# Gelu's tiles lent to MLP results, accumulator copies in halves, denominators spread a turn later, and TensorE's hand-over waits placed when due

## The chip, the cores and the metric

The kernel runs on one core of one Trainium2 chip. A core has a matrix engine (TensorE, PE in the profile, with its weight loads as PEld), a vector engine (VectorE, DVE), a scalar engine (ScalarE, ACT), GpSimd (POOL) and a sync engine (SyncE, SP), each with its own instruction queue that runs in order, and 16 DMA engines that move data between memory and the on-chip SBUF. TensorE writes to PSUM, which has 8 banks of 512 fp32 columns.

The metric is device time in microseconds of one execution. Of the kernel before there are three timed runs, and one more execution that was profiled.

## The reference

For x of 2048 tokens by 448 channels the reference computes an attention block and an MLP block on the same input and mixes them by a gate. Cut to what matters:

```python
def _A_ref(x, wqkv, wo):                 # S=2048, D=448, H=16 heads of Dh=28
    qkv = (x @ wqkv).reshape(B, S, 3, H, Dh)...
    scores = einsum("bhqd,bhkd->bhqk", q, k) * (Dh ** -0.5)
    p = softmax(scores)
    return einsum("bhqk,bhkd->bhqd", p, v)... @ wo

def _B_ref(x, w1, b1, w2, b2):           # F=1792
    y = layernorm(x)
    h = gelu(y @ w1 + b1)
    return h @ w2 + b2

g = sigmoid((x * gate_w).sum(-1, keepdims=True))
return g * _A_ref(x, ...) + (1 - g) * _B_ref(x, ...)
```

All of it is fp32. The kernel splits an operand a into a high part (rounded to a fast format, fp32r) and a low part a - high, and computes a product of two operands as high x high + high x low + low x high.

## The kernel before

**Two stages.** The first stage (class `Strips`, up to about 451 us) computes q, k, v, then the MLP, and beside them begins the row maxima of the attention scores. The second stage (from the loop over `turn_of`) computes scores, exponentials, the products with v, the projection and the mix.

**The strip stage.** TensorE's 128 rows are used as four row groups of 32 rows, "strips", that work side by side. Work is cut into pieces: `QK` and `Val` (q, k, v), `Up` (128 of the 1792 hidden channels for a block of 512 tokens) and `Down` (128 tokens of an MLP result). The 2048 tokens are four column blocks c = 0 to 3; in each 14 Up pieces are followed by 4 Down pieces. A piece owns one PSUM bank and must be visited once by each of the four strips, one after the other, since all four add into the same bank. The loop `run` is a planner: it keeps a planned time `t[s]` for each strip, takes the strip with the least time, and writes out one product at a time, with planned costs (0.232 us for a product of 512 columns, 0.204 for one of 448). This fixes the order of TensorE's instructions.

**Hand-overs.** When a strip has finished its visit, `end` lets SP increase a semaphore `hand` by one once the visit's last product is done, and keeps the count as `x.sig`. The piece counts as ready for another strip `HOP` = 0.6 us after the planned end (`x.ready`). The next strip's first product of that piece waits for `hand >= x.sig` (lines 486 and 487). SP's queue also holds DMA issues, and is in order.

**Row maxima.** Between these products each strip computes score products for the row maxima (line 212): 128 queries by 512 keys into bank 6 or 7, which VectorE then reduces (line 214). There are 1024 of them; those that the strip stage has no room for are done in attention by `lone`, up to three in a turn.

**Closing a piece.** `Up.close` lets ScalarE compute Gelu into a tile `h` (two buffers) and round it into `hh`; GpSimd then forms the low part `hl` out of `h` and `hh`. `Down.close` lets ScalarE copy the bank into a tile (line 398) and issue a transfer of it to the memory tensor `gbs` (line 401). That tile is `gb`, with two buffers; for the last two results of the last column block alone it is a tile of Gelu's `h`. The last strip of a first Up piece is held back while Down pieces of the block before are open.

**Attention.** The 16 heads are four groups g of four heads, the queries four blocks c of 512: n = 4g + c counts 16 accumulations. A turn computes five to seven units (128 keys by 512 queries of one head: three products each, line 1166), lets ScalarE take the exponential of them in two portions (line 1170), inserts row maxima (`lone`), then runs what the agenda holds for that turn, then products with v (line 1178) into bank 7. In a turn of five units the row maxima stand at three places: the first in bank 6, the second in another bank, the third in bank 6 again; in a turn of six there are two, both in bank 6. When the last product of an accumulation n has been placed, `valued` calls `finish_a`: VectorE copies bank 7 into `ob` (line 1026), and SP issues a transfer that brings the four rows of denominators into a small tile `lt`. Two turns later `finish_b` lets VectorE take reciprocals, and SP issues a store of them to memory and four transfers that spread them over 32 rows each (`rc`). Two turns after that `finish_c` lets GpSimd multiply `ob` by `rc`. The last accumulation goes another way (`finish_last`).

Of the kernel before, what the change touches and what calls it, by code (L numbers as in the profile page):

```python
# [15 lines left out]
P = 128  # L16
# [3 lines left out]
DH = 28  # L20
F = 1792
NG = 4
CH = 512
NC = S // CH
# [11 lines left out]
def kernel(ctx: ExitStack, tc: tile.TileContext, xt, wqk, wv, wo, xk, w1, b1, w2, b2,  # L36
                          ident_d, sel_d, out):
    nc = tc.nc
# [21 lines left out]
    rls = dram.tile([NG * NC, 4, CH], F32, name="rls")  # L60
# [101 lines left out]
    class RowMax:  # L162
# [64 lines left out]
        def close(self, n):  # L227
            mf, mt = self.mf[n % 2], self.mt[n % 2]
            nc.vector.reduce_max(mf[:, 0:16], self.mx[n % 2].rearrange("p j i k -> p (j i) k"), axis=AX)
            nc.vector.transpose(mt, mf)  # L230
# [14 lines left out]
    hand = tc.alloc_semaphore("hand")  # L245
# [123 lines left out]
    class Down(Piece):  # L369
# [21 lines left out]
            return st.hready.get((self.c, f, p), 1e9) > now or self.c == 0 and st.w2ready.get(f, 1e9) > now  # L391

        def close(self, st, now):
            if self.c == NC - 1 and self.i > 1:
                gb = mhp[0].tile([P, CH], F32, name="h", bufs=2)[:, :D]
            else:
                gb = mhp[0].tile([P, D], F32, name="gb", bufs=2)
            nc.scalar.activation(gb, bk[:, self.bank, :D], AF.Copy)  # L398
            st.use("act", now + 0.2, 0.56)
            st.free[self.bank] = st.act + 0.1  # L400
            nc.scalar.dma_start(gbs[self.c * TPC + self.i], gb)
            st.use("act", now, 0.5)

    class Strips:


        def __init__(self, tiles):
            self.tiles = tiles
            self.t = [0.0] * 4
            self.visit, self.held = [None] * 4, [None] * 4  # L410
            self.feed, self.stat = Feed(self, []), Feed(self, bxr)
            self.live = []
            self.free = {b: 0.0 for b in range(6)}
            self.rm = {6: 0.0, 7: 0.0}
            self.dve = self.act = self.pool = -1.0
            self.clock = self.dma = -1.0
            self.tasks = []
            self.count = 0
            self.hot = [1e9] * 4
            self.hready, self.yready, self.xready, self.wready, self.w1ready, self.w2ready = {}, {}, {}, {}, {}, {}  # L420
            self.vready = 1e9
            self.did = {}
            self.handed = 0

        def use(self, engine, start, cost):
            setattr(self, engine, max(getattr(self, engine), start) + cost)
# [6 lines left out]
        def at(self, t, fn, **uses):  # L433
            self.tasks.append((t, self.count, fn, uses))
            self.count += 1
# [30 lines left out]
        def run(self):  # L466
            while self.tiles or self.live:
                s = min(range(4), key=lambda s: (self.t[s], s))
                now = self.t[s]
                self.run_tasks(now)  # L470
                if self.rowmax(s, now):
                    continue
                v = self.visit[s]
                if v is None or v[0].fixed and self.held[s] is None:
                    x = self.pick(s, now, v and v[0])
                    if x is not None:
                        x.busy = True
                        self.held[s] = v
                        v = self.visit[s] = [x, x.ops(s), 0]
                if v is None or v[0].lacks(self, v[2], now):  # L480
                    self.t[s] = now + 0.1
                    continue
                x, ops, m = v
                a, b = ops[m] if not x.fixed else (ops[m][0][ops[m][2]][ops[m][3], ops[m][4]], ops[m][1][ops[m][2]][ops[m][3]])
                n = b.shape[-1]
                if m == 0 and x.sig:
                    nc.tensor.wait_ge(hand, x.sig)
                mm = nc.tensor.matmul(bk[:, x.bank, :n], a, b, start=x.first, stop=(len(x.rem) == 1 and m == len(ops) - 1),  # L488
                                      skip_group_check=True)
                x.first = False  # L490
                self.t[s] = now + x.cost
                v[2] += 1
                if v[2] == len(ops):
                    self.visit[s], self.held[s] = self.held[s], None
                    self.end(x, s, mm)
# [397 lines left out]
    for i, key in enumerate(load):  # L893
        r = slots[i % 8]
# [14 lines left out]
    for b, m in enumerate((0, 3, 4)):  # L909
        x = QK(0, m)  # L910
# [32 lines left out]
    def turn_bank(i):  # L943
        return (i + shift) % 6
# [73 lines left out]

    pv = bk[:, 7]
    obs = {}  # L1020

    def finish_a(n):
        ob = ao.tile([P, CH], F32, name="ob", bufs=1)
        lt = ao.tile([P, CH // 32], F32, name="lt")
        obs[n] = ob, lt
        nc.vector.tensor_copy(ob, pv)  # L1026
        nc.sync.dma_start(lt, ob[DH:P:32, :])

    def finish_b(n):
        ob, lt = obs[n]  # L1030
        rc = ao.tile([P, CH], F32, name="rc", bufs=1)
        obs[n] = ob, rc
        nc.vector.reciprocal(lt, lt)
        r = rls[n]
        nc.sync.dma_start(r.rearrange("j (a b) -> (j a) b", b=CH // 32), lt)
        for j in range(4):
            nc.sync.dma_start(rc[32 * j:32 * j + 32], r[j].partition_broadcast(32))

    def finish_c(n):
        g, c = divmod(n, NC)  # L1040
        ob, rc = obs.pop(n)
        if g < NG - 1:
            nc.gpsimd.tensor_mul(ot[g][:, c * CH:(c + 1) * CH], ob, rc)
            return
        nc.gpsimd.tensor_mul(ob, ob, rc)
        split_o(g, c, ob)
# [53 lines left out]
    def valued(n, turn):  # L1100

        g, c = divmod(n, NC)
        if n == NG * NC - 1:
            finish_last(n)
            return
        finish_a(n)
        at(turn + 2, lambda: finish_b(n))
        at(turn + 4, lambda: finish_c(n))
        if g == NG - 1:
            for i in range(TPC):  # L1110
                tail.append((turn + 6 + i, c * TPC + i))
# [7 lines left out]
    def lone(s, b, turn):  # L1119
        if not rowmax.ready(s) or turn < cold[s]:  # L1120
            return
        for kind, n, j in rowmax.one(s, bk[:, b]):
            if kind == "q":
                at(turn + 1, lambda n=n, j=j: rowmax.load_q(n, j))
            elif kind == "k":
                at(turn + 1, lambda n=n, j=j: rowmax.load_k(n, j))
                cold[j] = turn + 5
            else:
                at(turn + 1, lambda n=n: rowmax.close(n))
                at(turn + 2, lambda n=n: rowmax.store(n))  # L1130

    def turn_of(u, turn):

        left = UNITS - u
        owed = rowmax.left()
        size = 5 if owed and owed > 2 * ((left - 104) // 6) + 6 * sixes[0] else 6
        sixes[0] = size == 6
        if not owed and not (tail and tail[0][0] <= turn + 1):
            size = 7
        size = min(left, size)  # L1140
        na = min(4 if size == 7 else 3, size)
        nb = size - na
        for x in range(u, u + size):
            n = x // 64
            if n not in begins:
                begins.add(n)
                begun(n, turn)
        extra = {5: ((0, 3, 6), (3, 1, 5), (5, 2, 6)), 6: ((0, 3, 6), (5, 2, 6))}.get(size, ())
        if size == 7:
            sevens.append(turn)  # L1150
        place = (lambda i: i) if sevens else turn_bank
        if turn in projected:
            extra = extra[1:]
        for half, first, count in ((0, 0, na), (1, na, nb)):
            for p in range(3):
                for x, o, b in extra:
                    if x == 3 * half + p:
                        lone((u + o) % 4, b if b == 6 else turn_bank(b), turn)
                for i in range(first, first + count):
                    n, k = divmod(u + i, 64)  # L1160
                    k, j = divmod(k, 4)
                    r = slice(32 * j, 32 * j + DH + (p == 0))
                    ks = slice(k * P, (k + 1) * P)
                    w = (khi, klo, khi)[p][n // NC]
                    q = (qh, qh, ql)[p][n % 3]
                    nc.tensor.matmul(bk[:, place(i)], w[r, ks], q[r], start=(p == 0), stop=(p == 2), skip_group_check=True)  # L1166
            if count:
                t = ap.tile([P, 4 - half, CH], F32, name=f"p{half}")
                b = place(first)
                nc.scalar.activation(t[:, :count], bk[:, b:b + count], AF.Exp, scale=SCALE)  # L1170
                for i in range(count):
                    prob[u + first + i] = t[:, i]
        return size

    def batch(b, turn, sl=slice(0, CH)):
# [11 lines left out]
    while b < UNITS // 4:  # L1187
# [12 lines left out]
        while 4 * b + 4 <= before and quota:  # L1200
# [7 lines left out]
            b, begun_half = b + 1, False  # L1208
# [59 lines left out]
```

## Time and profile before

| | us |
|---|---|
| median of three runs | 1082.11 |
| lowest, highest | 1080.81, 1086.48 |
| the profiled execution | 1083.55 |
| its span, first to last instruction | 1081.8 |
| TensorE busy | 1068.8 (99%) |
| VectorE busy | 740.8 (68%) |
| ScalarE busy | 634.0 (59%) |
| GpSimd busy | 368.3 (34%) |
| granted TensorE clock | 0.999 |

A row of a group reads: line of the kernel, engine, operation, tile written <- tiles read, shapes, count; then busy time in us and mean duration in ns, and the idle time of the engine just before these instructions with what ended it ("<-"). A row of a timeline begins with the start and the length in us; several merged instructions carry a count. ACTq, SPq, DVEq and PEldq are an engine's queue: DMA issues and semaphore instructions, which are not counted as busy. TensorE's busy time covers up to four row groups that run side by side, so that 99% does not mean full speed.

### The profile page before, as it was taken

Reading aid. Unit: us, or ns where it says so; the run is one execution under the profiler, and the core shown is the slowest. Engines: PE = TensorE matmul, PEld = TensorE weight load, DVE = VectorE, ACT = ScalarE, POOL = GpSimd, SP = SyncE. Lnnn points to the kernel's source line nnn. Section 1 sums busy time; section 2 is a strip of 40 time slices with the busy share of each in tenths; the row PEclk is TensorE's granted clock in tenths of the full one; section 3 lists DMA queues with packets and bytes.
Section 4 is the critical chain, followed back from the end, with each engine's and each line's share of the span. In section 5 each row is a group of like instructions: output and inputs, shape, how many; then the busy total and the mean of one; then the engine's idle time right before and its main releaser. Section 6 shows DMA issues by size and latency. Waiting matters only on the chain.

```text
span 1081.8 us, 31072 instructions
## 1 busy us (share of the span) xinstructions
PE 1068.8 (99%) x13450; PEld 725.4 (67%) x13450; DVE 740.8 (68%) x1186; ACT 634.0 (59%) x654; POOL 368.3 (34%) x388
## 2 busy tenths in 40 slices
PE   9999999999999999999999999999999999999997
PEld 6999999999999899844444444444444444464555
DVE  4899998999999999876667655676664444422102
ACT  5234463042142033288788788778888888857671
POOL 4565577336244037441001101300110332444431
PEclk9999999999999999999999999999999999999999
DMA  6696433212100104220000011310000301011111
GB/s 232 214 269 217 168 111 104 77 46 61 45 7 7 46 12 118 92 77 18 25 11 27 16 31 38 78 41 6 25 26 23 71 27 50 25 55 36 61 47 67
DMA packets 47785, 73.20 MB, mean 68 GB/s; under 512 B 13840, under 2 KB 28816, under 8 KB 46848
## 3 DMA queue, kind: packets, MB, share of 16 engines
q1 hardware_dynamic: 33888, 39.11, 12.4%
q0 software_dynamic: 5120, 16.89, 5.5%
q10 hardware_dynamic: 8640, 15.21, 3.9%
q8 instruction: 105, 1.72, 0.7%
q14 instruction: 32, 0.26, 0.1%
HBM read 51.75 MB, written 19.31 MB: 66 GB/s over the span
## 4 chain that ended last, share of the span: by engine, by line
PE 95%; ACT 2%; DMA 2%; DVE 1%; issue 1%; SPq 0%; DVEq 0%; ACTq 0%
PE bk L488 34%; PE bk L1178 22%; PE bk L1166 18%; PE bk L212 15%; PE bk L1004 1%; ACT p L1170 1%; PE bk L1005 1%; PE bk L1006 1%; DMA gbs<-gb 1%; PE bk L920 1%; DMA first<-in_xt 1%; ACT gb L398 0%; DVE ob L1026 0%; PE bk L948 0%; DVE mx L214 0%
## 5 line engine op out<-in xcount | busy, mean ns | idle before, releaser
L214 DVE TENSOR_REDUCE mx<-bk 128x1 f32<-128x512 f32 x1024 | 673.7, 688 | 221.8 <-PE bk L212 178.6
L1170 ACT ACTIVATE p<-bk 128x1536 f32<-128x1536 f32 (+1 forms) x381 | 481.1, 1315 | 125.8 <-PE bk L1166 125.1
L212 PE MATMUL bk<-kd,qd 28*128 28x512 f32 x1024 | 449.8, 441 | 0.6 <-DVE mx L214 0.2
L212 PEld LDWEIGHTS bk<-kd,qd 28*128 28x128 f32 x1024 | 186.0, 182 | 179.7 <-DVE mx L214 115.1
L488 PE MATMUL bk<-yh,w1f 32*128 32x512 f32 x1568 | 192.9, 393 | 2.2 <-ACT gb L398 2.2
L488 PE MATMUL bk<-yl,w1f 32*128 32x512 f32 x784 | 167.4, 392 | 0.0
L488 PEld LDWEIGHTS bk<-yh,w1f 32*128 32x128 f32 x1568 | 154.6, 183 | 4.9 <-ACT gb L398 3.4
L488 PE MATMUL bk<-w2h,hh 32*128 32x448 f32 x896 | 145.0, 366 | 0.0
L488 PE MATMUL bk<-w2l,hh 32*128 32x448 f32 x896 | 144.1, 363 | 0.0
L1178 PE MATMUL bk<-p,va 128*32 128x512 f32 (+1 forms) x1144 | 130.2, 556 | 0.0
L1178 PE MATMUL bk<-p,vb 128*32 128x512 f32 (+1 forms) x1184 | 129.2, 542 | 0.0
L363 POOL TENSOR_TENSOR hl<-h,hh 128x512 fp32r<-128x512 f32 x56 | 72.4, 1305 | 137.2 <-ACT hh L356 99.7
L840 POOL CAST yh<-yl 128x512 fp32r<-128x512 f32 x16 | 9.8, 611 | 288.0 <-DMA yl<-qk 131.2
L488 PEld LDWEIGHTS bk<-yl,w1f 32*128 32x128 f32 x784 | 105.8, 183 | 0.3
L488 PEld LDWEIGHTS bk<-w2l,hh 32*128 32x128 f32 x896 | 103.1, 183 | 0.3
L488 PEld LDWEIGHTS bk<-w2h,hh 32*128 32x128 f32 x896 | 102.7, 183 | 0.4
L1166 PE MATMUL bk<-yh,ka 29*128 29x512 f32 x512 | 101.1, 483 | 0.5 <-ACT p L1170 0.5
L1166 PE MATMUL bk<-yh,kb 29*128 29x512 f32 x512 | 96.5, 480 | 1.7 <-ACT p L1170 1.7
L488 PE MATMUL bk<-w2h,hl 32*128 32x448 f32 x896 | 93.1, 362 | 0.0
L398 ACT ACTIVATE gb<-bk 128x448 f32<-128x448 f32 x14 | 7.6, 545 | 136.8 <-PE bk L488 129.7
L1166 PE MATMUL bk<-yh,la 28*128 28x512 f32 x512 | 83.4, 393 | 0.0
L488 PEld LDWEIGHTS bk<-w2h,hl 32*128 32x128 f32 x896 | 82.4, 183 | 0.3
(141 smaller groups left out, 1604.5 us busy)
## 6 DMA issues: line engine op xcount, KB each, us to landing
qk<-qo ACTq DMA_DIRECT2D x28, 256.0 KB
raw<-in_xt SPq DMA_DIRECT2D x17, 256.0 KB
vs<-vt ACTq DMA_DIRECT2D x16, 256.0 KB
rc<-rls SPq DMA_DIRECT2D x60, 64.0 KB
bxr<-in_xk POOLq DMA_DIRECT2D x8, 448.0 KB, 6.4
acc<-gbs SPq DMA_DIRECT2D x16, 224.0 KB
out_y<-acc SPq DMA_DIRECT2D x16, 224.0 KB
qd<-qk SPq DMA_DIRECT2D x60, 56.0 KB
```

Source lines behind the costliest of these rows:

```text
L212: nc.tensor.matmul(ps, self.qd[n % 2][r, i * P:(i + 1) * P], self.kd[r, k * 512:(k + 1) * 512], start=True, stop=True)
L214: nc.vector.reduce_max(self.mx[n % 2][:, j, i, k:k + 1], ps, axis=AX)
L363: nc.gpsimd.tensor_sub(hl[f], h, hh[f].bitcast(F32))
L488: mm = nc.tensor.matmul(bk[:, x.bank, :n], a, b, start=x.first, stop=(len(x.rem) == 1 and m == len(ops) - 1), skip_group_check=True)
L840: nc.gpsimd.tensor_copy(h, l.bitcast(F32))
L920: nc.tensor.matmul(bk[:, b], w, v, start=(i == 0), stop=(i == len(ops) - 1), skip_group_check=True)
L1004: nc.tensor.matmul(po, h, woh[:, g], start=(g == 0), stop=False, skip_group_check=True)
L1005: nc.tensor.matmul(po, h, wol[:, g], start=False, stop=False, skip_group_check=True)
L1006: nc.tensor.matmul(po, l, woh[:, g], start=False, stop=(g == NG - 1), skip_group_check=True)
L1166: nc.tensor.matmul(bk[:, place(i)], w[r, ks], q[r], start=(p == 0), stop=(p == 2), skip_group_check=True)
L1170: nc.scalar.activation(t[:, :count], bk[:, b:b + count], AF.Exp, scale=SCALE)
L1178: nc.tensor.matmul(bk[32 * j:32 * j + 32, 7, sl], vg[n // NC][:, k, 32 * j:32 * j + 32], prob[4 * b + j][:, sl], start=(k == 0), stop=(k = ...
```

## The change

There are four parts.

1. `Down.close` takes a tile of Gelu's `h` for the third and fourth token tile (i > 1) of every column block, where before it did so in the last block alone.
2. In `run` each strip product looks for the highest `sig` among all pieces whose planned `ready` has come (and its own piece's), and waits for it if TensorE has not waited for as much before (`passed`). Before, only the first product of a visit waited, for its own piece.
3. `finish_a` copies the first 256 columns of bank 7; the other 256 and the transfer of the denominators are put off to `copy_rest`, which the next turn calls behind its first row maximum (or at the end of its scores if it has none).
4. The four spreading transfers move out of `finish_b` into `spread_rc`, one turn later.

```diff
         def close(self, st, now):
-            if self.c == NC - 1 and self.i > 1:
+            if self.i > 1:
                 gb = mhp[0].tile([P, CH], F32, name="h", bufs=2)[:, :D]
             else:
                 gb = mhp[0].tile([P, D], F32, name="gb", bufs=2)
...
-            self.handed = 0
+            self.handed = self.passed = 0
...
-                if m == 0 and x.sig:
-                    nc.tensor.wait_ge(hand, x.sig)
+                due = max((y.sig for y in self.live if y.sig and y.ready <= now), default=0)
+                due = max(due, x.sig or 0)
+                if due > self.passed:
+                    nc.tensor.wait_ge(hand, due)
+                    self.passed = due
...
+    late = []
 
     def finish_a(n):
...
-        nc.vector.tensor_copy(ob, pv)
-        nc.sync.dma_start(lt, ob[DH:P:32, :])
+        nc.vector.tensor_copy(ob[:, :CH // 2], pv[:, :CH // 2])
+
+        def rest():
+            nc.vector.tensor_copy(ob[:, CH // 2:], pv[:, CH // 2:])
+            nc.sync.dma_start(lt, ob[DH:P:32, :])
+
+        late.append(rest)
+
+    def copy_rest():
+        while late:
+            late.pop()()
 
     def finish_b(n):
...
-        r = rls[n]
-        nc.sync.dma_start(r.rearrange("j (a b) -> (j a) b", b=CH // 32), lt)
+        nc.sync.dma_start(rls[n].rearrange("j (a b) -> (j a) b", b=CH // 32), lt)
+
+    def spread_rc(n):
         for j in range(4):
-            nc.sync.dma_start(rc[32 * j:32 * j + 32], r[j].partition_broadcast(32))
+            nc.sync.dma_start(obs[n][1][32 * j:32 * j + 32], rls[n][j].partition_broadcast(32))
...
         at(turn + 2, lambda: finish_b(n))
+        at(turn + 3, lambda: spread_rc(n))
         at(turn + 4, lambda: finish_c(n))
...
                         lone((u + o) % 4, b if b == 6 else turn_bank(b), turn)
+                        copy_rest()
...
+        copy_rest()
         return size
```

The order of TensorE's products is the same before and after; only waits move. On ScalarE, at the third crossing (the Down results of column block 2, then the first Gelus of block 3), the rows of before are these; a DMAHW wait is one for a transfer, Pool one for GpSimd:

```order
L398 ACTIVATE gb<-bk 128x448 [waits DMAHW2_49,PE_49]
L401 DMA gbs<-gb 128x448 [waits DMAHW6_49,Activation_49]
L398 ACTIVATE gb<-bk 128x448 [waits DMAHW3_49,PE_49]
L401 DMA gbs<-gb 128x448 [waits DMAHW7_49,Activation_49]
L398 ACTIVATE gb<-bk 128x448 [waits DMAHW6_49,PE_49]
L401 DMA gbs<-gb 128x448 [waits DMAHW0_49,Activation_49]
L398 ACTIVATE gb<-bk 128x448 [waits DMAHW7_49,PE_49]
L401 DMA gbs<-gb 128x448 [waits DMAHW1_49,Activation_49]
L355 ACTIVATE h<-bk,b1s 128x512 [waits PE_49,Pool_49]
```

and those of after:

```order
L398 ACTIVATE gb<-bk 128x448 [waits DMAHW0_49,PE_49]
L401 DMA gbs<-gb 128x448 [waits DMAHW6_49,Activation_49]
L398 ACTIVATE h<-bk 128x448 [waits PE_49,Pool_49]
L401 DMA gbs<-h 128x448 [waits DMAHW7_49,Activation_49]
L398 ACTIVATE h<-bk 128x448 [waits PE_49,Pool_49]
L401 DMA gbs<-h 128x448 [waits DMAHW0_49,Activation_49]
L398 ACTIVATE gb<-bk 128x448 [waits DMAHW2_49,PE_49]
L401 DMA gbs<-gb 128x448 [waits DMAHW1_49,Activation_49]
L355 ACTIVATE h<-bk,b1s 128x512 [waits DMAHW7_49,PE_49]
L356 ACTIVATE hh_2908<-h 128x512 [waits Activation_49]
L355 ACTIVATE h<-bk,b1s 128x512 [waits DMAHW0_49,PE_49]
```

The third and the fourth copy no longer wait for transfers issued in the same crossing (DMAHW6 and DMAHW7); the first two Gelus now wait for two of them (DMAHW7 and DMAHW0).

On VectorE, around the end of an accumulation in attention, before (mx is the tile of row maxima, x6 means six reductions in a row):

```order
L230 STREAM_TRANSPOSE mt_158<-mf_156 128x32
L214 TENSOR_REDUCE mx_155<-bk 128x1 x33
L1026 COPY ob<-bk 128x512
L214 TENSOR_REDUCE mx_155<-bk 128x1 x6
L1033 RECIPROCAL lt<-lt 128x16
```

and after:

```order
L230 STREAM_TRANSPOSE mt_158<-mf_156 128x32
L214 TENSOR_REDUCE mx_155<-bk 128x1 x33
L1030 COPY ob<-bk 128x256
L214 TENSOR_REDUCE mx_155<-bk 128x1
L1033 COPY ob<-bk 128x256
L214 TENSOR_REDUCE mx_155<-bk 128x1 x5
L1046 RECIPROCAL lt<-lt 128x16
```

One reduction now stands between the two halves.

On TensorE, a place in the Up products of the strip stage (w1f is a split weight tile, its number names the piece; yh and yl are the parts of y), before:

```order
L212 MATMUL bk<-kd,qd_153 128x512 [waits DVE_49]
L488 MATMUL bk<-yl,w1f_1773 128x512
L488 MATMUL bk<-yh,w1f_1744 128x512
L488 MATMUL bk<-yl,w1f_1629 128x512
L488 MATMUL bk<-yh,w1f_1773 128x512
L488 MATMUL bk<-yl,w1f_1744 128x512
L488 MATMUL bk<-yh,w1f_1688 128x512 [waits hand]
```

and after (the same pieces, under numbers that are lower by one to three):

```order
L212 MATMUL bk<-kd,qd_153 128x512 [waits DVE_49]
L491 MATMUL bk<-yl,w1f_1772 128x512 [waits hand]
L491 MATMUL bk<-yh,w1f_1742 128x512
L491 MATMUL bk<-yl,w1f_1627 128x512
L491 MATMUL bk<-yh,w1f_1772 128x512
L491 MATMUL bk<-yl,w1f_1742 128x512
L491 MATMUL bk<-yh,w1f_1685 128x512 [waits hand]
```

A product in the middle of another piece's visit (1772) now waits for a hand-over that is due.

## The prediction

> **What bounds the kernel now.** I read the page first: the engines' shares and the chain of waits.
>
> ```profile
> span 1081.8 us, 31072 instructions
> PE 1068.8 (99%) x13450; PEld 725.4 (67%) x13450; DVE 740.8 (68%) x1186; ACT 634.0 (59%) x654; POOL 368.3 (34%) x388
> PE 95%; ACT 2%; DMA 2%; DVE 1%; issue 1%; SPq 0%; DVEq 0%; ACTq 0%
> ```
>
> TensorE looks like the only bound. But its 99% is made of row groups that overlap, so I split the span by stage with the table of windows (columns: stretch, length, then busy time and count of PE, PEld, DVE, ACT, POOL).
>
> ```profile
> 60.00:182.00 122.00, 122.00 (x2064) 116.91 (x2063) 113.16 (x185) 58.16 (x115) 81.08 (x89) 1.00 0.55 176
> 182.00:451.00 269.00, 266.75 (x4601) 254.44 (x4593) 261.18 (x412) 68.40 (x111) 110.18 (x96) 1.00 0.16 46
> 451.00:1000.00 549.00, 546.57 (x5415) 256.95 (x5417) 314.69 (x497) 442.71 (x356) 118.32 (x116) 1.00 0.14 39
> ```
>
> In the strip stage (to 451 us) VectorE is busy 93% and then 97% of the time with row maxima: TensorE may place the next L212 product only when VectorE has emptied one of two banks. There VectorE sets the pace, and what counts is time in which VectorE idles. In attention (from 451) it is busy 57% and TensorE sets the pace, but each turn holds a chain through one bank: L212 product, row maximum, next L212 product.
>
> **Gelu's buffers.** The copies of the Down results (L398) use two buffers `gb`; the third must wait until the first one's transfer has landed. The view of that tile (what its engine waited for, then who waited for it), and the page's row of the products that wait:
>
> ```profile
> L398 ACT ACTIVATE gb<-bk x14: 543/545/547, 207.0 to 450.0; 128x448 f32<-128x448 f32 x14
>   DMA gbs<-gb: 6.7, 4
>   PEld bk L488: 3.4, 3
> L488 PE MATMUL bk<-yh,w1f 32*128 32x512 f32 x1568 | 192.9, 393 | 2.2 <-ACT gb L398 2.2
> ```
>
> ScalarE waited four times, 6.7 us in all, and three times TensorE waited for it (2.2 us with no product running, 3.4 us by its weight loads). ScalarE's timeline at the second and third crossing from one column block to the next:
>
> ```profile
> 290.22 0.33 ACTq L401 DMA_DIRECT2D gbs<-gb  x1
> 292.90 0.54 ACT L398 ACTIVATE gb<-bk 128x448 f32<-128x448 f32 x1 [1.71 <-DMA gbs<-gb]
> 297.48 0.69 ACT L355 ACTIVATE h<-bk,b1s 128x512 f32<-128x512 f32 x1 [0.61 <-PE bk L488]
> ...
> 371.88 0.33 ACTq L401 DMA_DIRECT2D gbs<-gb  x1
> 372.88 0.33 ACTq L401 DMA_DIRECT2D gbs<-gb  x1
> 376.03 0.54 ACT L398 ACTIVATE gb<-bk 128x448 f32<-128x448 f32 x1 [3.18 <-DMA gbs<-gb]
> 378.97 0.69 ACT L355 ACTIVATE h<-bk,b1s 128x512 f32<-128x512 f32 x1 [2.39 <-PE bk L488]
> ```
>
> What VectorE lost there: the same windows table for three stretches around the three waits (212.0 to 213.3, 291.9 to 294.6 and 374.9 to 377.5 us), its line of sums:
>
> ```profile
> sum 6.60, PE 4.36 PEld 3.15 DVE 3.20 ACT 2.36 POOL 0.00; mean PE 1.45 PEld 1.05 DVE 1.07 ACT 0.79 POOL 0.00
> ```
>
> VectorE idled 6.60 - 3.20 = 3.40 us; its usual 3% would be 0.2. With two of four results in `gb` and two in the Gelu tiles no copy waits for a transfer of its own crossing, so 3.2 us come back, and as VectorE is the pace, they reach the end. What is late next: the following block's first two Gelus must wait until those transfers have read the tiles. A transfer held its buffer from 371.88 to 376.03, 4.15 us, at worst, and from 290.22 to 292.90, 2.68 us, at the crossing before. Third crossing: the later of the two is issued at 372.88 and gone by 377.0; the first Gelu moves to about 378.97 - 1.9 = 377.1: nothing. Second: the fourth copy ends and issues near 293.3; the second Gelu moves to about 297.48 - 1.2 = 296.3, 3.0 us later: nothing by 2.68, 1.1 us by 4.15. I take 0.2, near the figure of the same place. Term: -3.0 us; ends -1.5 (2.2 us given back, 0.7 lost to Gelu) and -3.4.
>
> **Copies in halves.** Fifteen times VectorE copies a finished 512-column accumulator ahead of the turn's first row maximum. The tile's row, a row for 128 columns from the same memory, and the timeline of one such turn (531.35), of the next turn (534.32), and of a copy turn of another kind (830.65):
>
> ```profile
> L1026 DVE COPY ob<-bk x15: 690/692/692, 493.4 to 1023.5; 128x512 f32<-128x512 f32 x15
> L1071 DVE TENSOR_TENSOR ob<-ob,bk 128x128 f32<-128x128 f32 x4 | 1.1, 281 | 2.1 <-PE bk L1068 2.1
> ...
> 531.35 0.50 PE L212 MATMUL bk<-kd,qd 28*128 28x512 f32 x1
> 531.55 0.69 DVE L1026 COPY ob<-bk 128x512 f32<-128x512 f32 x1 [0.38 <-PE bk L1178]
> 532.16 1.96 DVE L214 TENSOR_REDUCE mx<-bk 128x1 f32<-128x512 f32 x3
> 532.27 0.61 SPq L1027 DMA_DIRECT2D lt<-ob  x1
> 532.89 0.50 PE L212 MATMUL bk<-kd,qd 28*128 28x512 f32 x1
> 534.32 0.49 PE L212 MATMUL bk<-kd,qd 28*128 28x512 f32 x1
> 534.85 2.00 DVE L214 TENSOR_REDUCE mx<-bk 128x1 f32<-128x512 f32 x3 [0.73 <-PE bk L212]
> 535.60 0.49 PE L212 MATMUL bk<-kd,qd 28*128 28x512 f32 x1
> 536.77 0.24 DVE L1033 RECIPROCAL lt<-lt 128x16 f32<-128x16 f32 x1
> ...
> 830.65 0.50 PE L212 MATMUL bk<-kd,qd 28*128 28x512 f32 x1
> 832.20 0.50 PE L212 MATMUL bk<-kd,qd 28*128 28x512 f32 x1
> ```
>
> An undisturbed turn has 535.60 - 534.32 = 1.28 us from its first bank-6 product to its second: 0.53 until the row maximum starts (534.85), 0.75 from there to the product. With the copy ahead it is 1.54, and 1.55 at 830.65: 0.26 us of TensorE each. No row shows a 256-column copy. On a line from 128 columns (0.281) to 512 (0.691) it takes 0.418; instructions in a row overlap by 0.08 (the copy is 0.69 long, the next starts after 532.16 - 531.55 = 0.61), so the next starts after 0.34; ends are 0.31, half of 0.61, and 0.42, no overlap. I take 0.35, nearest the line. Then the maximum starts at 531.90 instead of 532.16, and the second bank-6 product comes 0.25 us sooner. But the other half follows that maximum and pays its fixed part again. VectorE's chain is 531.55 + 0.35 + 0.65 + 0.35 + 0.65 + 0.69 = 534.24 (maxima 0.65 apart, 2.00 for three), and the next turn's product waits for the last maximum: about 534.30 against 534.32. In such short turns (three maxima, one group of four accumulations behind them: five of the fifteen) only 0.02 comes back. In eight turns with more accumulations or fewer maxima 0.25 does; two copies (899.9 and 1023.5 us) held up no second product. Term: 8 x 0.25 + 5 x 0.02 = -2.1 us; ends -0.9 (no overlap: 0.18 in eight turns, 0.1 lost in five) and -3.4 (13 x 0.26).
>
> [...]
>
> **Denominators.** The transfer of the sums (532.27) now follows the second half, 0.7 us later. The reciprocal that needs it stands two turns on, at 536.77. How fast it can land, from the last case, where VectorE had nothing else to do:
>
> ```profile
> 1024.23 0.56 SPq L1027 DMA_DIRECT2D lt<-ob  x1
> 1026.10 0.25 DVE L1033 RECIPROCAL lt<-lt 128x16 f32<-128x16 f32 x1 [1.89 <-DMA lt<-ob]
> ```
>
> 1.9 us after the issue, so 534.9 instead of 534.2 for a use at 536.8: hidden; with that cover gone VectorE would stand 0.7 us each time. The four spreading transfers go a turn later; on SP's queue they change places with other loads in three of fifteen cases, elsewhere nothing stands between. GpSimd's product waits for them, but GpSimd is 34% busy and its results are used turns later. Zero; 0.5 us either way.
>
> **Waits when due.** A piece handed to another row group needs SP's signal that its last product ended. Now TensorE waits where a visit starts; after, at the first strip product at which the planner counts the piece ready: earlier or at the same place, never later. The rows of the signals, of the separate wait instructions, and of transfers that SP issues between signals (first, longest single, last before the stage ends):
>
> ```profile
> L529 SPq EVENT_SEMAPHORE  x339: 17/17/17, 19.9 to 440.5; - x170
>   PEld bk L488: 0.4, 1
> L487 PEldq EVENT_SEMAPHORE  x36: 51/51/51, 33.9 to 429.3; - x36
> 60.28 3.58 SPq L196 DMA_DIRECT2D qd<-qk  x4
> 68.72 1.29 SPq L811 DMA_DIRECT2D ident<-in_ident  x1
> 409.84 40.88 SPq L196 DMA_DIRECT2D qd<-qk  x5
> ```
>
> All waits together cost 0.4 us today. The planner counts a piece ready 0.232 + 0.6 = 0.83 us after its last product's place; the product takes 0.39 (its row above), the signal 0.02, and weight load and way of the signal, which no row splits off, some part of the remaining 0.42; I leave half of it, 0.2, as margin. That is enough unless SP is just issuing a transfer: 86 of them between 60 and 451 us. At about 0.45 us that is a tenth of the time, so some 30 signals are held, by 0.1 us beyond the margin as a mean, 3 us of TensorE, with the 1.29 us at 68.72 as the worst single one. Behind a waiting product stand all four row groups, L212 among them, and so VectorE; but small stops are shorter than the row maximum that VectorE still has queued. I count a third, 0.9 us. Ends: -0.5 (ten fewer waits at 0.05) and +4.0 (all of it, and 1 us before 60).
>
> **Sum.** -3.0 - 2.1 + 0 + 0.9 = -4.2 us. The profiled execution took 1083.55 us (span 1081.8), 1.44 above the median of 1082.11. So 1079.35 by its own time and 1077.9 as a median, -0.4%. A measurement of this kernel can tell about 0.5% (5.4 us) from no change.
>
> **Rivals.** *Slower: early waits starve TensorE.* Its queue is in order; if each of some 300 moved waits cost the 0.051 us of a separate wait, that is 15 us against 5.1 won: 1092. It breaks even at 17 ns a wait and reaches +0.5% at 35 ns. For it: the margin of 0.2 us is only some four products long. Against it: 339 waits cost 0.4 us now, and VectorE's pace covers small stops. Chance 0.15. [...]
>
> *More: the waits are wholly covered* by VectorE's pace and the halves bring 0.25 in all thirteen turns: -3.2 - 3.3 = -6.5 us, 1075.6. For it: 93 and 97% busy; against: the short turns' chain. Chance 0.32. *The halves bring nothing,* because VectorE's longer chain ends the turn in more than five: -2.1 us, 1080.0; chance 0.10. The forecast has the remaining 0.43.
>
> **How the numbers follow.** Faster by over 0.5%: the second rival and a little of the forecast, 0.35. Slower: 0.15. Within: 0.50. The forecast alone reaches from 1076.0 to 1081.0; to hold eight in ten the range takes in the second rival and the worst of the waits short of starvation, 1074.0 to 1085.0. The slower case and little else stay out.
>
> **What would show it.** Buffers: no ScalarE wait on `gbs`, the 3.4 us of VectorE idle gone from the three crossings; wrong if Gelu waits for `gbs` and TensorE for Gelu. Halves: 1.29 us between bank-6 products in copy turns; wrong if these turns keep their length. Waits: L529 as releaser of L488 under 1.5 us in all; wrong if the stretch 60 to 182 us grows by several us with VectorE idle spread over it. If the strip stage ends later than at 451 us, the waits have eaten the buffers' gain, and the forecast is wrong.

## The result

Six executions of the kernel after have a median of 1078.53 us (1077.63 to 1080.01), six of the kernel before (the three timed ahead of the prediction among them) 1083.38 us. The ratio is 0.9959, with a 95% interval from 0.9946 to 0.9973: faster by 0.4%. The interval leaves out 1, and so does that of a later comparison, in five executions, 0.9954 (0.9940 to 0.9968). So a change of 0.4% can be told here; the prediction had put that limit at 0.5%. The profiled execution took 1077.71 us. Its page begins, and its chain of waits reads:

```profile
span 1075.9 us, 31093 instructions
PE 1065.5 (99%) x13450; PEld 726.0 (67%) x13450; DVE 740.5 (69%) x1201; ACT 633.3 (59%) x654; POOL 367.7 (34%) x388
...
PE 97%; ACT 1%; issue 1%; DMA 0%; DVE 0%; DVEq 0%; SPq 0%; ACTq 0%
```

The 15 more VectorE instructions are the second halves. In the chain ScalarE and the transfers, 2% each before, have shrunk to 1% and 0. The table of windows for the same stretches as before (stretch, length, then busy time and count of PE, PEld, DVE, ACT, POOL):

```profile
60.00:182.00 122.00, 121.97 (x2059) 116.88 (x2056) 112.10 (x185) 57.74 (x115) 81.21 (x89) 1.00 0.56 175
182.00:451.00 269.00, 268.90 (x4619) 257.01 (x4613) 261.90 (x413) 70.04 (x112) 109.80 (x96) 1.00 0.17 49
```

From 182 to 451 us TensorE now stands still for 0.10 us in place of 2.25, and more products (4619 against 4601) fit into the stretch.

**Where the time came from.** Both kernels give TensorE the same products in the same order, so the start of each weight load can be set against the start of the same one in the trace of before. The table gives how far each trace moved against that of before within a stretch (us; minus is time won; medians over a dozen loads at each end). The crossings are 211 to 260, 290 to 330 and 374 to 430 us of the trace of before; what is left out between them and attention is under 0.1 us, but for 1.35 in the row of the waits 0.6 us earlier. The rows below the first two are the experiments of the next section.

| kernel | 0 to 60 | 60 to 211 | crossing 1 | to 290 | crossing 2 | to 374 | crossing 3 | attention, 451 to 1000 | at the end |
|---|---|---|---|---|---|---|---|---|---|
| after | -0.38 | +0.36 | -0.66 | +0.39 | -1.13 | +0.10 | -1.76 | -2.81 | -5.85 |
| after, again | -0.06 | +0.23 | -0.65 | 0.00 | -1.06 | +0.04 | -1.78 | -2.70 | -5.99 |
| Gelu's buffers alone | -0.19 | +0.97 | -0.65 | +0.04 | -1.04 | -0.02 | -1.76 | +0.06 | -2.64 |
| halves alone | -0.10 | +0.75 | -0.05 | +0.02 | -0.59 | -0.03 | -0.09 | -2.70 | -2.79 |
| waits when due alone | -0.54 | +1.16 | -0.25 | +0.01 | -0.60 | +0.05 | -0.04 | -0.02 | -0.27 |
| after without waits when due | -0.13 | -0.03 | -0.74 | +0.04 | -1.07 | +0.05 | -1.71 | -2.79 | -6.34 |
| the same, again | -0.78 | +1.23 | -0.73 | +0.06 | -1.10 | +0.13 | -1.77 | -2.77 | -5.75 |
| waits 0.3 us earlier | +0.28 | +2.71 | +0.01 | +0.42 | -0.73 | +0.25 | -1.44 | -2.75 | -1.26 |
| waits 0.6 us earlier | +11.58 | +33.79 | +9.29 | +3.51 | +8.26 | +4.55 | +9.76 | -2.84 | +79.27 |
| whole copy, moved | -1.17 | +0.40 | -0.73 | +0.06 | -1.11 | +0.05 | -1.71 | -0.61 | -4.89 |

Read by columns it separates the parts. At the crossings the kernels with lent buffers win 3.4 to 3.6 us in all (the two with earlier waits left aside). The two that keep the old buffers move there too, by 0.73 us (halves alone) and 0.89 us (waits when due alone), most of it at the second crossing: the trace of before holds a long wait there, as the next section shows. Attention moves only where the copies are changed, and among the seven executions with halves it repeats within 0.15 us. The stretch from 60 to 211 us does not: its +0.36, -0.03 and +1.23 belong to no part of the change. Most of it arises at one place near 109 us, where a product of the v pieces starts late in some executions.

### The profile page after: what moved, and what is told of

Same layout as the page of the kernel before. It is cut to its first block, busy times and chain, and to the rows that moved or that the text cites. A ratio compares the mean times of both kernels' runs of the same rounds, so it can differ in the third digit from the quotient of the medians.

```text
span 1075.9 us, 31093 instructions
## 1 busy us (share of the span) xinstructions
PE 1065.5 (99%) x13450; PEld 726.0 (67%) x13450; DVE 740.5 (69%) x1201; ACT 633.3 (59%) x654; POOL 367.7 (34%) x388
## 4 chain that ended last, share of the span: by engine, by line
PE 97%; ACT 1%; issue 1%; DMA 0%; DVE 0%; DVEq 0%; SPq 0%; ACTq 0%
PE bk L491 35%; PE bk L1195 22%; PE bk L1182 19%; PE bk L212 15%; PE bk L1007 1%; ACT p L1186 1%; PE bk L1008 1%; PE bk L1009 1%; PE bk L923 1%; DMA first<-in_xt 0%; PE bk L951 0%; DVE acc L1014 0%; PE bk L908 0%; PE bk L1082 0%; PE bk L1076 0%
## 5 line engine op out<-in xcount | busy, mean ns | idle before, releaser
L1182 PE MATMUL bk<-yl,ka 28*128 28x512 f32 x512 | 82.1, 408 | 0.0
```

## The experiments

### One part at a time

The first three kernels are the kernel before with one part each. Gelu's buffers:

```diff
-            if self.c == NC - 1 and self.i > 1:
+            if self.i > 1:
```

> The kernel before with the Gelu buffers alone. By the prediction's term: -3.0 us against the kernel before, ratio 0.9972, no copy of a Down result waiting for a transfer, the strip stage ending 3 us sooner and attention as long as before. The two traces, read product by product, put -3.45 us on the three crossings, which would be 0.9968. Rival: the crossings gain only together with the waits when due (which let a block's first Gelu come sooner); then the buffers alone bring 1.5 us or less, ratio 0.9986 or more, and the first Gelus of blocks 1 to 3 wait for gbs.

Measured: 1080.60 us against 1083.00, -2.4 us, ratio 0.9977 (0.9967 to 0.9988). The three crossings brought 3.45 us, nearly what they brought in the kernel after (3.55 and 3.49), and no other stretch did. So the buffers need no help from the waits. What VectorE lost at the crossings before, and with the buffers, stands in the windows 211 to 215, 290 to 296 and 373 to 379 us, 16 us in all. The line of sums for the kernel before:

```profile
sum 16.00, PE 13.75 PEld 11.80 DVE 12.60 ACT 3.97 POOL 0.00; mean PE 4.58 PEld 3.93 DVE 4.20 ACT 1.32 POOL 0.00
```

and with the buffers lent, nothing else changed:

```profile
sum 16.00, PE 16.00 PEld 15.38 DVE 15.85 ACT 7.61 POOL 1.22; mean PE 5.33 PEld 5.13 DVE 5.28 ACT 2.54 POOL 0.41
```

VectorE was busy for 12.60 of 16 us and is for 15.85: 3.25 us. The table has 3.45 us for the crossings and no later stretch that takes them back, so they reach the end. The profiled execution of before was a bad one for this wait, however. Its windows in the kernels that keep the old buffers, the one with halves alone first and the one with waits when due alone after it, are these:

```profile
sum 16.00, PE 14.32 PEld 12.27 DVE 13.14 ACT 4.24 POOL 0.00; mean PE 4.78 PEld 4.09 DVE 4.38 ACT 1.41 POOL 0.00
```

```profile
sum 16.00, PE 14.53 PEld 12.63 DVE 13.35 ACT 4.66 POOL 0.00; mean PE 4.84 PEld 4.21 DVE 4.45 ACT 1.55 POOL 0.00
```

There VectorE lost 2.9 and 2.7 us, not 3.4, and the crossings were 0.73 and 0.89 us shorter than in the trace of before without any lent buffer. Against these two executions the buffers bring 3.45 - 0.73 = 2.7 and 3.45 - 0.89 = 2.6 us. At the second crossing the third copy waited like this in the kernel with halves alone:

```profile
290.81 0.33 ACTq L401 DMA_DIRECT2D gbs<-gb  x1
291.24 0.55 ACT L398 ACTIVATE gb<-bk 128x448 f32<-128x448 f32 x1 [0.46 <-PE bk L488]
291.81 0.33 ACTq L401 DMA_DIRECT2D gbs<-gb  x1
293.05 0.54 ACT L398 ACTIVATE gb<-bk 128x448 f32<-128x448 f32 x1 [1.26 <-DMA gbs<-gb]
```

1.26 us, where the quoted timeline of before has 1.71: the same transfer held its buffer for 2.24 us and not 2.68. The long waits of that one execution thus account for 0.7 to 0.9 us of the distance between 3.45 in the traces and 2.4 in the medians; the rest is within the interval.

The copies in halves alone (`finish_a`, `copy_rest` and its two calls as in the diff, the spreading transfers left in `finish_b`):

```diff
-        nc.vector.tensor_copy(ob, pv)
-        nc.sync.dma_start(lt, ob[DH:P:32, :])
+        nc.vector.tensor_copy(ob[:, :CH // 2], pv[:, :CH // 2])
...
+            nc.vector.tensor_copy(ob[:, CH // 2:], pv[:, CH // 2:])
+            nc.sync.dma_start(lt, ob[DH:P:32, :])
```

> The kernel before with the copies in halves alone (denominators spread where they were). By the prediction's term: -2.1 us, ratio 0.9981, eight turns 0.25 us shorter and five short ones 0.02. The traces of before and after, read turn by turn, say -2.8 us (0.9974), with 0.17 us in the short turns. Rival: VectorE's longer chain ends the turns, and the copies bring under 0.5 us (0.9995 or more).

Measured: 1081.05 us, -1.95 us, ratio 0.9979 (0.9968 to 0.9989). Attention was 2.70 us shorter, all of it in the copy turns, the same as in the kernel after to 0.02 us a turn. As the spreading transfers stay early here and are late there, moving them costs nothing and brings nothing.

The waits when due alone:

```diff
-                if m == 0 and x.sig:
-                    nc.tensor.wait_ge(hand, x.sig)
+                due = max((y.sig for y in self.live if y.sig and y.ready <= now), default=0)
+                due = max(due, x.sig or 0)
+                if due > self.passed:
+                    nc.tensor.wait_ge(hand, due)
+                    self.passed = due
```

> The kernel before with the waits when due alone. By the prediction's term: +0.9 us (ends -0.5 and +4.0), ratio 1.0008; the strip stage ends 1 us later, attention is as long as before. The traces of before and after say +0.4 us or nothing (1.0004 or less). Rival of starvation: +15 us, ratio 1.014, with SP's signals named as releaser of Up products for several us. Other rival: that the waits stand earlier saves time, -0.5 us.

Measured: 1082.65 us, -0.35 us, ratio 0.9988 (0.9977 to 0.9999). Starvation, at +15 us, is out. The interval ends just under 1, which speaks for a small gain; the two comparisons below have the other sign, so the sign stays open. The trace does not show a gain either: of the parts of its row in the table, -0.60 at the second crossing appears as -0.59 in the kernel with halves alone too, and is the shorter transfer (the third copy waits 1.25 us for it here, 1.26 in that kernel and 1.71 in the trace of before).

The kernel after with that part taken back (the same diff, reversed):

> The kernel after with the waits put back to the visit's first product; Gelu's buffers, halves and the later spread stay. By the prediction's terms: -5.1 us against the kernel before, ratio 0.9953, which is 0.9 us less than the kernel after. By the traces: -6.2 us, 0.9943. If the waits when due cost nothing at all, it takes the same time as the kernel after (0.9959 in its own comparison, with an interval from 0.9946 to 0.9973); if they help, it is slower than that.

Measured: 1078.21 us, ratio 0.9953 (0.9935 to 0.9970); strip stage and attention won 3.56 and 2.79 us. The three parts alone sum to -2.4 - 1.95 - 0.35 = -4.7 us, and the whole change was -4.85 and -4.67 in its two comparisons: within these intervals they neither help nor disturb each other.

To settle whether the waits cost or save anything, the two kernels ran side by side once more. First the kernel after:

> The kernel after once more, beside the one without the waits when due, so that the two share one chip and the same runs of the kernel before. Its ratio should fall into the interval that it had (0.9946 to 0.9973).

and the one without waits when due:

> The kernel after with the waits back at the visit. The run with waits 0.3 us earlier paid 4.6 us for 46 us of early waits, a tenth; a tenth of the 2.3 us in the kernel after is 0.2 us, so the two medians should lie within 0.5 us of each other, this one lower by 0.2 if at all. By the prediction's term it is 0.9 us lower. If the waits when due save time in themselves, as the lower ratio of the run with them alone might say, it is some 0.4 us higher.

Measured: 1078.15 us (1077.03 to 1078.69) and 1077.77 us (1076.36 to 1078.34), ratios 0.9954 and 0.9950. Without the waits when due the kernel is 0.38 us lower here and was 0.32 lower before, across two sets of runs. The executions overlap almost wholly, and the run with the waits alone had the other sign, so a cost of 0.3 to 0.4 us is possible, and not shown.

### How much of an early wait is paid

The prediction took a third of the stops, and gave VectorE's pace as the reason. Two kernels make the stops larger, by counting a hand-over as due earlier than the planner's ready time:

```diff
-                due = max((y.sig for y in self.live if y.sig and y.ready <= now), default=0)
+                due = max((y.sig for y in self.live if y.sig and y.ready - 0.3 <= now), default=0)
```

> The kernel after, but a hand-over counts as due 0.3 us before the planner's ready time, so that TensorE's waits stand some 0.3 us earlier. Set against the signals of the trace of before, 306 of 321 waits now come before their signal, by 46 us in all (7.5 until 60 us, 18.5 until 182 us, 20 until 451 us); in the kernel after it was 2.3 us. If VectorE's pace covers small stops (the prediction's reason, a third shows), 15 us or less of it reach the end, and in the stretch 182 to 451 us next to nothing. If each stop is paid in full, the time is 46 us above the kernel after, some 1124 us, and the stretches grow by 18 and 20 us.

In the second one HOP (0.6) stands in place of 0.3.

> The same with 0.6 us: TensorE waits for each signal right behind the visit that gives it. Set against the signals of the trace of before, all 330 waits come early, by 157 us in all (23, 59 and 76 us in the three stretches). Stops of half a microsecond are no longer shorter than the row maxima that VectorE has queued (0.65 us each), so the cover should break: if it covers a fixed part of each stop, the share paid is clearly higher than in the run with 0.3 us; if a third is paid whatever the size, +52 us; paid in full +157 us.

Measured: 1082.29 and 1162.82 us, in one execution each; the traces are compared. Against the kernel after, the strip stage grew by 1.51 + 3.06 = 4.6 us of 46, and by 82.09 + 3.06 = 85.1 us of 157: a tenth and 54%, and nearly these shares in each of the three stretches. The paid share is thus no constant. A constant length fits both: if the first 0.22 us of every stop are free and the rest is paid, the stops worked out for the expectations (each wait's new place in the trace of before, against the time of its signal there) give 4.2 us for the first kernel and 85.0 for the second. By stretches (to 60, 182 and 451 us) the fit is looser: about 0.9, 2.5 and 0.8 us by the rule for the first kernel, where 0.7, 2.1 and 1.8 were measured, and 13, 32 and 39 for the second, against 12, 31 and 43. For the kernel after, whose 28 early waits come 2.3 us too soon in all, the same rule gives 0.6 us, against the 0.3 to 0.4 of the medians.

Busy times for 20 to 451 us, of the kernel after, then with 0.3 us, then with 0.6 us:

```profile
sum 431.00, PE 430.87 PEld 412.96 DVE 405.78 ACT 138.77 POOL 214.88; mean PE 143.62 PEld 137.65 DVE 135.26 ACT 46.26 POOL 71.63
```

```profile
sum 431.00, PE 430.93 PEld 402.53 DVE 405.23 ACT 136.16 POOL 214.93; mean PE 143.64 PEld 134.18 DVE 135.08 ACT 45.38 POOL 71.64
```

```profile
sum 431.00, PE 426.92 PEld 329.99 DVE 343.51 ACT 118.30 POOL 177.18; mean PE 142.31 PEld 110.00 DVE 114.50 ACT 39.43 POOL 59.06
```

With 0.3 us VectorE kept its pace (405.2 of 431 us), though weight loads ran for 10 us less; with 0.6 us it fell to 343.5. The profile does not name the small stops. Who waited for SP's signals, in the kernel after, with 0.3 and with 0.6 us:

```profile
  PEld bk L491: 0.7, 2
```

```profile
  PEld bk L491: 3.1, 11
```

```profile
  PEld bk L491: 72.0, 219
```

3.1 us in 11 waits, where 306 came early: most of the small stops leave no row. They did happen: in the trace with 0.3 us itself some 260 of the 321 weight loads that wait start within 0.06 us of their signal, in the kernel after some 50 of 324. What the free 0.22 us consist of is not shown.

### Is it the halves, or only their place?

The kernel after, with the whole copy behind the first row maximum:

```diff
-        nc.vector.tensor_copy(ob[:, :CH // 2], pv[:, :CH // 2])
-
         def rest():
-            nc.vector.tensor_copy(ob[:, CH // 2:], pv[:, CH // 2:])
+            nc.vector.tensor_copy(ob, pv)
             nc.sync.dma_start(lt, ob[DH:P:32, :])
```

> The kernel after, with the whole copy behind the first row maximum in place of two halves around it. If only the place ahead of the first row maximum cost time, it takes as long as the kernel after: 1.28 us between bank-6 products in copy turns, each turn as short as with halves. If the halves are needed, because the products with v wait for the end of the copy (0.07 us after the second half in the kernel after) and VectorE's chain for the next turn is longer by 0.27 us, the eleven copy turns that gained give back about 0.27 to 0.33 us each: +3.0 us against the kernel after, attention no shorter than before the change, although its bank-6 products stand 1.28 us apart.

Measured: 1078.67 us in its one execution, too few to set beside the medians. In its trace attention won 0.61 us in place of 2.8: the halves are needed. The same short turn in the kernel after, VectorE and then TensorE's products for row maxima and with v (the first row begins the turn before, one without a copy):

```profile
528.36 0.42 DVE L1030 COPY ob<-bk 128x256 f32<-128x256 f32 x1 [0.40 <-PE bk L1195]
528.70 0.68 DVE L214 TENSOR_REDUCE mx<-bk 128x1 f32<-128x512 f32 x1
529.30 0.41 DVE L1033 COPY ob<-bk 128x256 f32<-128x256 f32 x1
529.63 1.28 DVE L214 TENSOR_REDUCE mx<-bk 128x1 f32<-128x512 f32 x2
```

```profile
525.44 0.50 PE L212 MATMUL bk<-kd,qd 28*128 28x512 f32 x1
...
528.16 0.49 PE L212 MATMUL bk<-kd,qd 28*128 28x512 f32 x1
...
529.44 0.49 PE L212 MATMUL bk<-kd,qd 28*128 28x512 f32 x1
...
529.87 1.07 PE L1195 MATMUL bk<-p,va 128*32 128x512 f32 x8
530.97 0.50 PE L212 MATMUL bk<-kd,qd 28*128 28x512 f32 x1
```

and with the whole copy, VectorE and then the weight loads of the same products:

```profile
528.33 0.68 DVE L1032 COPY ob<-bk 128x512 f32<-128x512 f32 x1
528.93 1.28 DVE L214 TENSOR_REDUCE mx<-bk 128x1 f32<-128x512 f32 x2
```

```profile
527.20 0.18 PEld L212 LDWEIGHTS bk<-kd,qd 28*128 28x128 f32 x1 [0.84 <-DVE mx L214]
...
528.47 0.18 PEld L212 LDWEIGHTS bk<-kd,qd 28*128 28x128 f32 x1 [0.18 <-DVE mx L214]
529.07 0.16 PEld L1194 LDWEIGHTS bk<-p,va 128*32 128x32 f32 x8 [0.41 <-DVE ob L1032]
530.26 0.18 PEld L212 LDWEIGHTS bk<-kd,qd 28*128 28x128 f32 x1 [1.04 <-DVE mx L214]
```

Both have 1.27 to 1.28 us between the bank-6 products, and yet the turn takes 530.97 - 528.16 = 2.81 us with halves and 530.26 - 527.20 = 3.06 with the whole copy. Two waits took the gain: the products with v wait 0.41 us for the copy, where a turn without a copy shows 0.25, and the next turn's product waits 1.04 us for the last row maximum, where 0.84 is usual. Four of the five short turns became 0.09 us longer than before the change, and most of the others kept 0.10 of their 0.27 (the wait of 0.41 us, 0.16 too long). The expectation had the two waits, and too high a price: +3.0 us against the kernel after, measured 2.2. (Its 0.07 us from the second half to the products with v is 0.15 in the trace of the kernel after: the half ends at 529.72, their first weight load starts at 529.87.)

## Why the prediction was right

1077.9 us were forecast; 1078.53 and 1078.15 were measured. The parts did what the prediction said, by the ways that it named, but their sizes were less exact than the sum.

**Gelu's buffers: -3.0, measured -3.45 in the traces, -2.4 in the medians.** The reading held at every step: no copy waits for a transfer of its own crossing, VectorE's idle time at the crossings is gone, and it reaches the end because VectorE is the pace (busy for 261.18 of the 269 us from 182 to 451 us before, 261.90 after). The 0.2 us for late Gelus did not arise. The view of `gbs` in the kernel after has no one that waited for these tiles but GpSimd's fetches in attention:

```profile
L401 ACTq DMA_DIRECT2D gbs<-gb x8: 326/326/327, 207.6 to 447.5; - x8
L401 ACTq DMA_DIRECT2D gbs<-h x8: 326/326/546, 211.3 to 449.5; - x8
...
  POOL acc L992: 36.2, 8
```

What the prediction did not have is that a wait for a transfer is one draw: 3.4 us in the execution it had, 2.7 and 2.9 in two others. Against those two the crossings won 2.6 and 2.7 us. (It moves the next block's Gelus by 1.9 us at the third crossing and 1.2 at the second, where VectorE's idle time in its windows is 1.74 and 1.10. Nothing hangs on it, as no Gelu waited for a transfer.)

**Copies in halves: -2.1, measured -2.7 in the traces, -1.95 in the medians.** The way was right, and the term was mis-sized in two places that partly cancel.

| copy turns | predicted, each | measured, each | sum, predicted | sum, measured |
|---|---|---|---|---|
| five short turns | 0.02 | 0.17 (four), 0.26 (one) | 0.10 | 0.94 |
| eight others | 0.25 | 0.27 (six), 0.17 (one), 0 (one) | 2.0 | 1.79 |

(Behind the short turn that won 0.26 us the next one lost 0.08 and the one after it won 0.09. With such small changes in other turns the rows agree with the 2.7 to 2.8 us of attention in the table of stretches.) In the short turns the step that failed was VectorE's chain, 531.55 to 534.24, 2.69 us. In the rows above it runs from 528.36 to 530.91, 2.55 us: the steps are 0.34, 0.60, 0.33 and 1.28 where the prediction has 0.35, 0.65, 0.35 and 1.34. It took 0.65 us for the distance from a maximum to the next instruction, both times. That was the mean over an undisturbed turn (534.85), where the second maximum starts only after the first has ended, 0.71 us behind its start; back to back the distance is 0.60. The last step, 0.06 us from the last maximum to the next turn's product, was right, and the chain still ends those turns: undisturbed ones take 2.72 us (525.44 to 528.16), these 2.81, and the one short turn that is followed by no row maximum got the full 0.26.

Of the eight others one gained nothing, although it shows the sign that the prediction named. Its products in the kernel after:

```profile
859.78 0.49 PE L212 MATMUL bk<-kd,qd 28*128 28x512 f32 x1
...
860.97 0.51 PE L1182 MATMUL bk<-yh,ka 29*128 29x512 f32 x3 [0.21 <-ACT p L1186]
861.07 0.49 PE L212 MATMUL bk<-kd,qd 28*128 28x512 f32 x1
```

1.29 us lie between the bank-6 products (1.55 at 865.08 before), but the turn waits for ScalarE's exponentials and takes 3.52 us in both kernels. The other, at 977 us before, kept 0.17. There the first weight load of the products with v stands 0.53 us behind the last one of the scores, where it stood 0.43 behind it before. The profile names the second half of the copy:

```profile
972.76 0.41 DVE L1033 COPY ob<-bk 128x256 f32<-128x256 f32 x1
973.43 0.16 PEld L1195 LDWEIGHTS bk<-p,vb 128*32 128x32 f32 x8 [0.34 <-DVE ob L1033]
```

But the second half ended at 973.17, 0.26 us before that load, while the load that waited for the whole copy above started 0.06 us after its end. So what took these 0.10 us is not shown. The distance between two products was the sign of a wait removed, not of time won.

The 256-column copy took 0.424 us and the next instruction started 0.34 us after its start; the prediction had 0.418 and 0.35. The near end of the term, -0.9 us, was the author's estimate for no overlap between instructions; the measured overlap of 0.08 us and the -2.7 us of the traces go against it here.

**Denominators: 0, measured 0.** The kernel with halves alone and the kernel after have the same attention to 0.11 us, and the same copy turns to 0.02.

**Waits when due: +0.9, measured between -0.35 and +0.4.** That they would cost little was right, and the reason too coarse: stops are not paid by a third but from about 0.22 us on, and few are so long. The prediction's 3 us of stops compare with the 2.3 worked out from the real places of the waits. Its margin of 0.2 us was a little too wide: in the trace of before the signal comes 0.67 us (median; 0.55 at the least) after the start of the visit's last weight load, which leaves 0.16 of the 0.83 us. SP's signal as releaser shows 0.7 us, under the 1.5 named.

**The rivals.** Starvation (+15 us) fell with the run of waits alone, and would have been real 0.6 us earlier (1162.82 us). "The halves bring nothing" fell. "More" (-6.5 us) was nearly right on the waits and wrong on the thirteen full turns; the traces, -5.85 us, came nearer to it than the medians did, but the long waits of the trace of before are in that figure.

**How near the sum came is in part luck.** By the medians alone the parts are -2.4, -1.95 and -0.35 us where -3.0, -2.1 and +0.9 were forecast: two gains were a little smaller, and the cost of the waits was missing. The whole gained 4.85 and 4.67 us, more than the 4.2 forecast. And the forecast started from 1082.11 us, the median of three runs, where the comparisons gave 1083.38 and 1082.82: a higher start and a larger gain partly cancel.

**What stays open.** The late start near 109 us, up to 1.2 us in some executions, is in kernels with and without each part; the trace names no releaser for it. None of the kernels is shown to beat the one after: without the waits when due it is 0.3 to 0.4 us lower, within the uncertainty.

## What to carry to other kernels

VectorE set the pace of the strip stage, its idle time at the crossings was the price of the waits for transfers, and it came back whole in the traces: 3.25 us more of VectorE, 3.45 us won (2.4 in the medians). But take a wait for a transfer from several executions, since a single profile can hold a long one: 3.4 us of VectorE lost in one execution, 2.9 and 2.7 in two others. Before you move or split an instruction on the engine between two others, list everyone who waits for its end, not only the one that waited until now: the whole copy freed the row maxima (1.27 us between the bank-6 products) and stopped the products with v (0.41 us of waiting in place of 0.25). Early waits in this queue cost a tenth of their length when they were 46 us in all and 54% when they were 157, so two or three sizes of delay tell more than one share.

## What the runs showed of the hardware

- Around the copies of the kernel after, VectorE instructions back to back overlapped by 0.08 us, also across kinds: at 528.36 us a 256-column copy of 0.424 us is followed after 0.34 us, the row maximum of 0.68 us behind it after 0.60. In the kernel before it was 0.08 us too, behind a 512-column copy of 0.69 us (531.55, followed at 532.16).
- Attention from 451 to 1000 us moved by -2.70 to -2.84 us against the trace of before in all seven executions with halves. The stretch from 60 to 211 us moved by -0.03 and +1.23 us against the trace of before in two executions of the same kernel. In the two kernels that were traced twice the columns of the table up to 290 us differ by 0.19 and 0.64 us in sum, the ends by 0.14 and 0.59.
- 46 us of early waits at the head of TensorE's queue (worked out against the signals in the trace of before) cost 4.6 us, and 157 us of them 85.1 us. A free length of about 0.22 us for each wait, fitted to these two kernels, gives both sums; in the last stretch, with VectorE 97% busy, it gives 0.8 us where 1.8 were measured.
